# Choosing experts with plain float32 logits on four column groups, scales spread by a transfer, transposes issued together

## The chip, the core and the metric

The kernel runs on one core of a Trainium2 chip. The metric is the device time of one execution in microseconds. The kernel before takes 819.78 us (median of 3 runs, 819.25 to 821.07). The execution that the profiler recorded took 818.29 us, and its span, from the first to the last instruction, is 816.4 us.

## What is computed

The reference chains three layers over 4 sequences of 576 tokens with 512 features. First comes linear attention with 8 heads, then a feed-forward layer with a hidden size of 2048, then a layer with 8 experts of hidden size 1024. Only the last one's choice of experts is touched here:

```python
logits = np.einsum('bsd,de->bse', x, w_gate)
local_gate = 1.0 / (1.0 + np.exp(-np.einsum('bsd,de->bse', x, w_local).squeeze(-1)))
for b in range(B):
    prev_e = -1
    for s in range(S):
        fresh_e = int(np.argmax(logits[b, s]))
        if s == 0 or local_gate[b, s] < 0.5:
            e = fresh_e
        else:
            e = prev_e if prev_e >= 0 else fresh_e
        prev_e = e
        ...
        h = np.maximum(x[b, s] @ w1[e], 0.0)
        out[b, s] = p[e] * (h @ w2[e])
```

A token takes the expert of the token before it unless its gate is below one half. So nearly all tokens of a sequence share one expert. The result of each token is scaled by p[e], a softmax of the logits.

## The kernel before, in words

Features lie on the 128 partitions in four groups, tokens along the free dimension. The array `y` holds the stream of 4 x 2304 values per partition.

**Attention** (lines 426 to 479) runs in 29 steps, `attn_step`. Each loads keys and queries from memory on SP (`load_kq`, line 231, two buffers) and projects them (`proj`, line 292).

**Feed-forward and experts** are made of blocks (lines 511 and 512). The feed-forward layer has four units of five blocks of 432 or 480 tokens. Each sequence has two expert units, `g` 0 and 1, of two blocks of 288 tokens. Every product is made of three matmuls in float32r: high by high, low by high and high by low halves (`mm1`, lines 525 to 527; `mm2`, lines 544 to 546; output `psf`). `split_rows` (line 493) makes the halves of 288 tokens on ACT and POOL. The weights of an expert come as 8 pieces per unit. SP loads a piece into one of two raw buffers (line 153), ACT makes its high half (line 172) and DVE its low half (line 176).

**The order of work** is written out by hand. `work()` (line 747) goes through the blocks. Each block is 8 pieces of 12 matmuls, and after each piece comes a call of `side()` (line 705). That call does one step of a background list `bg` and prepares at most a few weight pieces. `route(b)`, a generator, is in that list, and each `yield` ends one step. It is appended in blocks 2, 3 and 4 of the last feed-forward unit for sequences 0, 1 and 2, and in the first expert block for sequence 3. While sequence 0 is not chosen, two steps are done per call. In `route(b)`:

- lines 574 to 578: both halves of the sequence are split, then three empty steps;
- line 586: 16 float32r matmuls of 288 columns give the logits (`glps`), from the split tokens and from the gate's weights as high and low half side by side (`wgr`, 18 columns); two copies to `r_gl`, line 587;
- line 593: five products with 18 rows (`lgps`) add the halves and put tokens on the partitions;
- lines 608 to 627: argmax, gate and softmax as small DVE instructions on `tr`;
- line 636: five transposes (`trps`), two in one step and three in the next, the last of 64 rows;
- lines 642 to 648: a scan along the tokens finds the kept expert; the probabilities are split into `r_th` and `r_tl`;
- line 650: POOL's queue writes both into `sall` on 32 of 64 partitions;
- lines 654 to 670: the most frequent expert is found (`cps` is a transpose of 8 counts), and `r_pm` marks the row to use.

`scale_row(b)` is put in front of `bg` at the start of an expert unit. Through `spread` it makes a selecting matrix on TensorE (`selps`, line 685) and two products with `sall` (`sbps`, line 691). They are copied to `sbc` (line 692), by which POOL multiplies the result (line 556). A loop after all that (from line 843) handles tokens whose expert differs. In the recorded execution it makes no pass.

Of the kernel before, what the change touches and what calls it, by code (L numbers as in the profile page):

```python
# [7 lines left out]
F32 = mybir.dt.float32  # L8
# [30 lines left out]
def model(ctx, tc, kq, vx, wphi, ident, up, vp, wff, wg, wmoe, rconst, outT):  # L39
# [8 lines left out]
    h_p = right.enter_context(tc.tile_pool(name="h", bufs=5, side="right"))  # L48
    ula_p = ctx.enter_context(tc.tile_pool(name="ula", bufs=1))
# [6 lines left out]
    wg_sb = const.tile([128, 4, 9], F32, name="wg_sb")  # L56
    wgr = const.tile([128, 4, 18], F32R, name="wgr")
# [512 lines left out]
    def route(b):  # L570

        ps_r, ul_p = late["psr"], late["ul"]
        lg, tr = late["lg"], late["tr"]
        for c in range(2):
            split_rows(b, c)
            yield
        for _ in range(3):
            yield

        gl = row(S, "r_gl")[:18]  # L580
        for c in range(2):
            sl = slice(c * CH, (c + 1) * CH)
            ps = ps_r.tile([18, CH], F32, tag="r1", bufs=2, name="glps")
            for k in range(4):
                for part in range(2):
                    nc.tensor.matmul(ps, lhsT=wgr[:, k], rhs=halves(b * S + c * CH, CH)[part][:, k], start=(k + part == 0), stop=(k + part == 4))  # L586
            nc.vector.tensor_copy(out=gl[:, sl], in_=ps)
            yield
        yield
        ps = ps_r.tile([128, 5, 9], F32, tag="r0", name="lgps")  # L590
        for c in range(5):
            m = 128 if c < 4 else 64
            nc.tensor.matmul(ps[:m, c], lhsT=gl[:, c * 128:c * 128 + m], rhs=rc_sb[:18, 104:113], start=True, stop=True)
# [34 lines left out]
        for _ in range(2):  # L628
            yield
        ta, tk, tp = (row(S, "r_t" + nm)[:8] for nm in "akp")  # L630
        for s0, cs in ((0, (0, 1)), (256, (2, 3, 4))):
            ps = ps_r.tile([72, 320], F32, tag="r1", bufs=2, name="trps")
            w = 0
            for c in cs:
                m = 128 if c < 4 else 64
                nc.tensor.transpose(ps[:, w:w + m], tr[:m, c], id_sb[:m, :m])
                w += m
            for n_, t in enumerate((ta, tk, tp)):
                nc.vector.tensor_copy(out=t[:, s0:s0 + w], in_=ps[32 * n_:32 * n_ + 8, :w])
            yield  # L640
# [5 lines left out]
        th, tl = (row(S, "r_t" + nm)[:8] for nm in "hl")  # L646
        nc.vector.tensor_copy(out=th.bitcast(F32R), in_=tp)
        nc.vector.tensor_tensor(out=tl.bitcast(F32R), in0=tp, in1=th, op=ALU.subtract)
        for n_, t in enumerate((th, tl)):
            nc.gpsimd.dma_start(out=late["sall"][32 * n_ + 8 * b:32 * n_ + 8 * b + 8], in_=t.bitcast(F32R))  # L650
        for _ in range(4):
            yield
# [14 lines left out]

        pm = ul_p.tile([1, 64], F32, tag=f"r_pm{b}", name="r_pm")
        nc.vector.tensor_scalar(out=pf, in0=pf, scalar1=float(8 * b), scalar2=None, op0=ALU.add)
        one_of_32(pm, pf)  # L670
        place[b] = pm
        pidx[b] = ix

    place = {}

    def one_of_32(dst, at_):

        nc.vector.tensor_scalar(out=dst.rearrange("p (a n) -> p a n", a=2), in0=iota32[0:1].unsqueeze(1).to_broadcast([1, 2, 32]),
                                scalar1=at_, scalar2=None, op0=ALU.is_equal)

    def spread(dst, pm):

        ps_r, ul_p, ones1, sall = (late[n] for n in ("psr", "ul", "ones1", "sall"))
        ps = ps_r.tile([64, 128], F32, tag="r1", bufs=2, name="selps")
        nc.tensor.matmul(ps, lhsT=pm, rhs=ones1, start=True, stop=True)
        sel = ul_p.tile([64, 128], F32R, tag="r_sel", name="r_sel")
        nc.vector.tensor_copy(out=sel, in_=ps)
        yield
        for c in range(2):
            ps = ps_r.tile([128, CH], F32, tag="r1", bufs=2, name="sbps")  # L690
            nc.tensor.matmul(ps, lhsT=sel, rhs=sall[:, c * CH:(c + 1) * CH], start=True, stop=True)
            nc.vector.tensor_copy(out=dst[:, c * CH:(c + 1) * CH], in_=ps)
            yield

    def scale_row(b):
        t = late["ul"].tile([128, S], F32, tag="sbc", name="sbc")
        scale[b] = t
        yield from spread(t, place[b])
# [16 lines left out]
    def side(i, step):  # L715

        u, _, _, c = blocks[i]
        if u.kind == "ffn":
            if splits and step in (2, 6):
                split_rows(*splits.pop(0))  # L720
            if u.g < 3:
                for _ in range(2 if step in (3, 7) else 1):
                    if not preps and room() and at["prep"] < min(8 * u.g + 16, 8 * u.g + 10 + 8 * c // 5 if u.g else 16):
                        preps.append(w_prep())
                    prep_step()
                if late:
                    w_ahead()
            else:
                if step == 0 and c > 1:
                    bg.append(route(c - 2))  # L730
                bg_step()
                if 0 not in pidx:
                    bg_step()
                if 0 in pidx and step in (1, 3, 4, 5, 7):
                    if at["prep"] < 8 * len(ffn_units) + 8 and room():
                        preps.append(w_prep())
                        drain(preps)
                        w_ahead()
        else:
            k = units.index(u)  # L740
            if u.b == 0 and u.g == 0 and c == 0 and step == 0:
                bg.append(route(3))
            bg_step()
            if c == 0 and step == 4 and u.g == 0:
                bg.insert(0, scale_row(u.b))
            if k + 1 < len(units) and at["prep"] < min(8 * (k + 2), 8 * k + 8 + 4 * c + (step + 1) // 2) and room():
                v = units[k + 1]
                if v.b not in pidx:
                    drain(bg)
                preps.append(w_prep())  # L750
                drain(preps)
                w_ahead()

    def work():

        for f in range(4):
            mm1(0, f)
            yield
        for i in range(n):
            u = blocks[i][0]  # L760
            if u.kind == "moe" and u.g == 1 and u.b not in scale:
                drain(bg)

            first = 3 if i == 1 else 0
            if i + 1 < n and not first:
                mm1(i + 1, 0)
            side(i, 0)
            yield
            for d in range(4):
                if first and d == first:  # L770
                    mm1(i + 1, 0)
                mm2(i, d)
                side(i, 1 + d)
                yield
            if i + 1 < n:
                for f in range(1, 4):
                    mm1(i + 1, f)
                    if f > 1:
                        store(1)
                    side(i, 4 + f)  # L780
                    yield
# [9 lines left out]
    def prepare(S_, late_):  # L791

        if (S_, late_) in ((1, 1), (2, 1), (3, 0), (4, 0)):
            next(early[0], "end")
        if late_ and S_ == W0:
            nc.vector.tensor_copy(out=wgr[:, :, 0:9], in_=wg_sb)
            nc.vector.tensor_tensor(out=wgr[:, :, 9:18], in0=wg_sb, in1=f32(wgr[:, :, 0:9]), op=ALU.subtract)
            w_dma()
        if S_ > W0:
            if S_ % 2 and late_ and at["prep"] < 8:  # L800
                preps.append(w_prep())
                w_ahead()
            prep_step()

    for S_ in range(NALL):
        if S_ == 1:
            nc.sync.dma_start(out=rc_sb, in_=rconst)
            nc.sync.dma_start(out=wg_sb, in_=wg)
        attn_step(S_)
# [7 lines left out]
    late["sall"] = ul_p.tile([64, S], F32R, name="sall")  # L817
# [10 lines left out]
    nc.gpsimd.memset(f32(late["sall"]), 0.0)  # L828
# [13 lines left out]
    with tc.For_i(0, nl):  # L842
# [3 lines left out]
        po = l_p.tile([1, 64], F32, name="l_po")  # L846
        be = l_p.tile([1, 2], F32, name="l_be")
        pl = l_p.tile([1, 4, 2], F32, name="l_pl")
        bi = l_p.tile([1, 6], I32, name="l_bi")
# [4 lines left out]
        one_of_32(po, pf)  # L854
        nc.vector.tensor_tensor(out=flags, in0=flags, in1=po[:, 0:32], op=ALU.subtract)
# [15 lines left out]
        nc.vector.tensor_copy(out=bi[:, 0:2], in_=be)  # L871
        nc.vector.tensor_copy(out=bi[:, 2:6], in_=pl[:, 0:2].rearrange("p a c -> p (a c)"))
        ev = nc.sync.value_load(bi[0:1, 1:2], min_val=0, max_val=NE - 1)
        bs = nc.sync.value_load(bi[0:1, 0:1], min_val=0, max_val=B - 1)
        bv = nc.vector.value_load(bi[0:1, 0:1], min_val=0, max_val=B - 1)
# [3 lines left out]
        for _ in spread(ls, po):  # L879
            pass  # L880
# [41 lines left out]
def layout(inputs):  # L922
# [41 lines left out]
    rc[0:18, 104:113] = np.concatenate([np.eye(9), np.eye(9)])  # L964
# [27 lines left out]
```

## Time and profile before

| what | value |
|---|---|
| median of 3 runs | 819.78 us |
| the profiled execution | 818.29 us |
| its span | 816.4 us |
| PE (TensorE matmul) busy | 797.6 us, 98% |
| DVE, ACT, POOL busy | 56%, 33%, 23% |
| TensorE clock granted, mean | 0.997 |

A line of a view names the engine, the line of the kernel, the operation, output and inputs by their names, partitions by elements, and a count. PE stands for matmuls, PEld for the loading of weights, SPq for the queue of SP. Matmuls are pipelined: the duration shown for one is longer than the distance to the next, so distances between starts tell what one costs in a stream.

### The profile page before, as it was taken

The numbers are of one execution on the slowest core, as the hardware profiler recorded it, in microseconds if no ns is written. First come the engines' busy times: TensorE is split into PE (matmuls) and PEld (weight loads), VectorE is DVE, ScalarE is ACT, GpSimd is POOL, SyncE is SP. The second block draws the span as 40 slices with busy tenths as digits, with TensorE's granted clock in tenths as the row PEclk, the third lists the DMA queues.
The fourth block names the chain that finished last, engine by engine and source line by source line (L and its number), as shares of the span: only waits on it lengthen the run. The fifth ranks groups of instructions, "written<-read, shape, count | busy, mean of one in ns | idle before, by whom it ended". The sixth has DMA issues, their size and how long they took to land.

```text
span 816.4 us, 17943 instructions
## 1 busy us (share of the span) xinstructions
PE 797.6 (98%) x7528; PEld 729.9 (89%) x7528; DVE 460.9 (56%) x913; ACT 267.5 (33%) x589; POOL 185.1 (23%) x242
## 2 busy tenths in 40 slices
PE   7999999999999999999999999999999999999995
PEld 5998889999888999889998899878899989999995
DVE  7899898732775453535545352247564847634332
ACT  5767776642311111111111111202233242333330
POOL 1122332100662221212212120023005232202011
PEclk9999999999999999999999999999999999999998
DMA  6434343100111110101101000002122322424311
GB/s 192 146 119 145 120 135 113 62 2 1 53 52 51 52 52 27 52 26 52 52 26 52 27 1 1 0 1 67 53 67 78 114 81 66 138 78 120 107 41 68
DMA packets 24676, 54.90 MB, mean 67 GB/s; under 512 B 3152, under 2 KB 8272, under 8 KB 24592
## 3 DMA queue, kind: packets, MB, share of 16 engines
q1 hardware_dynamic: 20304, 49.52, 19.4%
q10 hardware_dynamic: 4032, 4.05, 1.4%
q8 instruction: 61, 1.00, 0.5%
q0 software_dynamic: 256, 0.15, 0.1%
q14 instruction: 23, 0.19, 0.1%
HBM read 48.84 MB, written 4.72 MB: 66 GB/s over the span
## 4 chain that ended last, share of the span: by engine, by line
PE 90%; DVE 4%; ACT 2%; DMA 1%; issue 1%; POOL 1%; SPq 0%; DVEq 0%; ACTq 0%
PE psf L525 12%; PE psf L544 12%; PE psf L545 12%; PE psf L546 12%; PE psf L526 12%; PE psf L527 12%; PE kv L327 4%; PE pj L292 4%; PE num L361 3%; PE tq L341 2%; PE tps L387 1%; PE utps L404 1%; PE glps L586 1%; PE utps L399 1%; DMA kq<-in_kq 1%
## 5 line engine op out<-in xcount | busy, mean ns | idle before, releaser
L544 PE MATMUL psf<-hhi,w 128*128 128x288 f32 (+2 forms) x576 | 195.4, 339 | 0.5 <-ACT w L172 0.5
L545 PE MATMUL psf<-hhi,w 128*128 128x288 f32 (+2 forms) x576 | 194.3, 337 | 0.3 <-DVE w L176 0.3
L546 PE MATMUL psf<-hlo,w 128*128 128x288 f32 (+2 forms) x576 | 194.4, 337 | 0.0
L531 DVE SCALAR_TENSOR_TENSOR hlo<-psf,hhi 128x288 fp32r<-128x288 f32 (+2 forms) x144 | 80.0, 556 | 181.4 <-ACT hhi L530 181.2
L530 ACT ACTIVATE hhi<-psf 128x288 fp32r<-128x288 f32 (+2 forms) x144 | 70.8, 492 | 259.7 <-PE psf L527 256.1
L525 PE MATMUL psf<-hi_b,w 128*128 128x480 f32 (+1 forms) x352 | 120.8, 343 | 0.0
L526 PE MATMUL psf<-lo_b,w 128*128 128x480 f32 (+1 forms) x352 | 120.4, 342 | 0.1
L527 PE MATMUL psf<-hi_b,w 128*128 128x480 f32 (+1 forms) x352 | 119.9, 341 | 0.0
L544 PEld LDWEIGHTS psf<-hhi,w 128*128 128x128 f32 x576 | 108.2, 188 | 8.1 <-ACT w L172 0.8
L545 PEld LDWEIGHTS psf<-hhi,w 128*128 128x128 f32 x576 | 108.3, 188 | 7.2 <-DVE w L176 0.5
L553 DVE TENSOR_TENSOR y<-psf,y 128x480 f32<-128x480 f32 (+2 forms) x112 | 65.5, 585 | 87.1 <-PE psf L546 86.6
L546 PEld LDWEIGHTS psf<-hlo,w 128*128 128x128 f32 x576 | 108.2, 188 | 6.8
L75 POOL TENSOR_TENSOR cv_w<-cv_w,cv_b 128x256 f32<-128x256 f32 x64 | 45.9, 739 | 228.9 <-DVE cv_b L91 188.9
L525 PE MATMUL psf<-hi_a,w 128*128 128x432 f32 (+1 forms) x224 | 75.0, 335 | 0.0
L527 PE MATMUL psf<-hi_a,w 128*128 128x432 f32 (+1 forms) x224 | 74.1, 331 | 0.0
L526 PE MATMUL psf<-lo_a,w 128*128 128x432 f32 (+1 forms) x224 | 73.9, 330 | 0.0
L525 PEld LDWEIGHTS psf<-hi_b,w 128*128 128x128 f32 x352 | 66.1, 188 | 6.8 <-issue 0.5
L526 PEld LDWEIGHTS psf<-lo_b,w 128*128 128x128 f32 x352 | 66.1, 188 | 6.7 <-POOL lo_b L500 1.4
L527 PEld LDWEIGHTS psf<-hi_b,w 128*128 128x128 f32 x352 | 66.1, 188 | 5.2
L176 DVE TENSOR_TENSOR w<-raw,w 128x512 fp32r<-128x512 f32 x64 | 44.9, 701 | 29.8 <-ACT w L172 29.1
L172 ACT CAST w<-cv_w 128x512 fp32r<-128x512 f32 x32 | 19.9, 623 | 122.3 <-POOL cv_w L75 105.1
L556 POOL TENSOR_TENSOR y<-y,sbc 128x288 f32<-128x288 f32 x30 | 29.6, 988 | 133.2 <-DVE y L553 129.8
(139 smaller groups left out, 1151.4 us busy)
## 6 DMA issues: line engine op xcount, KB each, us to landing
raw<-in_wff SPq DMA_DIRECT2D x32, 512.0 KB, 3.3
raw<-in_wmoe SPq DMA_DIRECT2D x64, 256.0 KB, 2.7
kq<-in_kq SPq DMA_DIRECT2D x15, 576.0 KB, 4.1
vt<-in_vx SPq DMA_DIRECT2D x16, 325.0 KB, 3.0
outT<-y ACTq DMA_DIRECT2D x27, 144.0 KB, 3.0
outT<-y SPq DMA_DIRECT2D x5, 144.0 KB, 1.8
kq<-in_kq SPq DMA_DIRECT2D x2, 192.0 KB, 3.3
rawc<-in_up SPq DMA_DIRECT2D x1, 160.0 KB, 5.6
```

The costliest lines, as they stand in the source:

```text
L75: eng.tensor_tensor(out=dst[:, sl], in0=a[:, sl], in1=b[:, sl], op=op)
L176: nc.vector.tensor_tensor(out=w[:, 1], in0=f, in1=f32(w[:, 0]), op=ALU.subtract)
L292: nc.tensor.matmul(ps[c:c + 64, n_, i], lhsT=raw[g][r, t0 + c:t0 + c + 64], rhs=wphi_sb[r], start=True, stop=True)
L525: nc.tensor.matmul(ps, lhsT=wh, rhs=hi[:, k], start=(k == 0), stop=False)
L526: nc.tensor.matmul(ps, lhsT=wh, rhs=lo[:, k], start=False, stop=False)
L527: nc.tensor.matmul(ps, lhsT=wl, rhs=hi[:, k], start=False, stop=(k == 3))
L530: nc.scalar.activation(out=hhi, in_=ps, func=ACTF.Relu)
L531: nc.vector.scalar_tensor_tensor(out=hlo, in0=ps, scalar=0.0, in1=f32(hhi), op0=ALU.max, op1=ALU.subtract)
L544: nc.tensor.matmul(ps, lhsT=wh, rhs=hhi, start=(f == 0), stop=False)
L545: nc.tensor.matmul(ps, lhsT=wl, rhs=hhi, start=False, stop=False)
L546: nc.tensor.matmul(ps, lhsT=wh, rhs=hlo, start=False, stop=(f == 3))
L553: nc.vector.tensor_tensor(out=dst, in0=ps, in1=dst, op=ALU.add)
```

## The change

The logits come from `y` itself in plain float32. For each half of a sequence the four feature groups go to four groups of 32 output partitions, one matmul each. The gate's weights are padded with zeros to 32 columns. The five products that follow have 128 rows and add the four groups. The splits of the tokens move behind the logits (first half) and behind the softmax (second half). All five transposes are full and stand in one step. `route` has 16 steps where it had 21.

The probabilities go unsplit to memory on SP's queue, twice (`mine`, `sall`). The scale is loaded from `mine` by one SP transfer that repeats the chosen row on 128 partitions. `spread`, `one_of_32`, `selps` and `sbps` are gone. The load of the gate's weights stands outside of the `if`: it is issued ahead of every attention step.

```diff
-    wg_sb = const.tile([128, 4, 9], F32, name="wg_sb")
-    wgr = const.tile([128, 4, 18], F32R, name="wgr")
+    wg_sb = const.tile([128, 4, 32], F32, name="wg_sb")
...
-        for c in range(2):
-            split_rows(b, c)
-            yield
-        for _ in range(3):
-            yield
-
-        gl = row(S, "r_gl")[:18]
+        yield
+
+        gl = row(S, "r_gl")
         for c in range(2):
-            sl = slice(c * CH, (c + 1) * CH)
-            ps = ps_r.tile([18, CH], F32, tag="r1", bufs=2, name="glps")
+            ps = ps_r.tile([128, CH], F32, tag="r1", bufs=2, name="glps")
+            t0 = b * S + c * CH
             for k in range(4):
-                for part in range(2):
-                    nc.tensor.matmul(ps, lhsT=wgr[:, k], rhs=halves(b * S + c * CH, CH)[part][:, k], start=(k + part == 0), stop=(k + part == 4))
-            nc.vector.tensor_copy(out=gl[:, sl], in_=ps)
-            yield
+                nc.tensor.matmul(ps[32 * k:32 * k + 32], lhsT=wg_sb[:, k], rhs=y[:, k, t0:t0 + CH], start=True, stop=True)
+            nc.vector.tensor_copy(out=gl[:, c * CH:(c + 1) * CH], in_=ps)
+        yield
+        split_rows(b, 0)
+        yield
         yield
...
-            nc.tensor.matmul(ps[:m, c], lhsT=gl[:, c * 128:c * 128 + m], rhs=rc_sb[:18, 104:113], start=True, stop=True)
+            nc.tensor.matmul(ps[:m, c], lhsT=gl[:, c * 128:c * 128 + m], rhs=rc_sb[:, 104:113], start=True, stop=True)
...
-        for _ in range(2):
-            yield
+        yield
+        split_rows(b, 1)
+        yield
...
-            ps = ps_r.tile([72, 320], F32, tag="r1", bufs=2, name="trps")
+            ps = ps_r.tile([72, 384], F32, tag="r1", bufs=2, name="trps")
             w = 0
             for c in cs:
-                m = 128 if c < 4 else 64
-                nc.tensor.transpose(ps[:, w:w + m], tr[:m, c], id_sb[:m, :m])
-                w += m
+                nc.tensor.transpose(ps[:, w:w + 128], tr[:, c], id_sb)
+                w += 128
+            w = min(w, S - s0)
             for n_, t in enumerate((ta, tk, tp)):
                 nc.vector.tensor_copy(out=t[:, s0:s0 + w], in_=ps[32 * n_:32 * n_ + 8, :w])
-            yield
+        yield
...
-        th, tl = (row(S, "r_t" + nm)[:8] for nm in "hl")
-        nc.vector.tensor_copy(out=th.bitcast(F32R), in_=tp)
-        nc.vector.tensor_tensor(out=tl.bitcast(F32R), in0=tp, in1=th, op=ALU.subtract)
-        for n_, t in enumerate((th, tl)):
-            nc.gpsimd.dma_start(out=late["sall"][32 * n_ + 8 * b:32 * n_ + 8 * b + 8], in_=t.bitcast(F32R))
-        for _ in range(4):
+        yield
+
+        mine[b] = dram.tile([8, S], F32, name=f"mine{b}")
+        nc.sync.dma_start(out=mine[b], in_=tp)
+        nc.sync.dma_start(out=late["sall"][8 * b:8 * b + 8], in_=tp)
+        for _ in range(3):
             yield
...
     def scale_row(b):
-        t = late["ul"].tile([128, S], F32, tag="sbc", name="sbc")
-        scale[b] = t
-        yield from spread(t, place[b])
+
+        scale[b] = late["ul"].tile([128, S], F32, tag="sbc", bufs=2, name="sbc")
+        nc.sync.dma_start(out=scale[b], in_=mine[b][bass.ds(ereg[b], 1)].partition_broadcast(128))
...
             if c == 0 and step == 4 and u.g == 0:
-                bg.insert(0, scale_row(u.b))
+                scale_row(u.b)
...
         if late_ and S_ == W0:
-            nc.vector.tensor_copy(out=wgr[:, :, 0:9], in_=wg_sb)
-            nc.vector.tensor_tensor(out=wgr[:, :, 9:18], in0=wg_sb, in1=f32(wgr[:, :, 0:9]), op=ALU.subtract)
             w_dma()
...
     for S_ in range(NALL):
         if S_ == 1:
             nc.sync.dma_start(out=rc_sb, in_=rconst)
-            nc.sync.dma_start(out=wg_sb, in_=wg)
+            nc.gpsimd.memset(wg_sb[:, :, 9:32], 0.0)
+        nc.sync.dma_start(out=wg_sb[:, :, 0:9], in_=wg)
         attn_step(S_)
```

Left out are the loop for the tokens of other experts, the constants that pick the four groups, and the removed helpers' bodies.

## Rows read from the trace of the kernel before

**Rows 1.** Page, part 1: busy time of each engine, share of the span.
```profile
PE 797.6 (98%) x7528; PEld 729.9 (89%) x7528; DVE 460.9 (56%) x913; ACT 267.5 (33%) x589; POOL 185.1 (23%) x242
```
**Rows 2.** Busy time by stretch: PE, PEld, DVE, ACT, POOL, then clock, DMA.
```profile
585.00:640.00 55.00, 55.00 (x400) 52.49 (x399) 34.18 (x95) 20.81 (x44) 11.70 (x14) 1.00 0.26 77
```
**Rows 3.** Waits of PE: us in total, times, longest us.
```profile
PE psf L544 <- ACT w L172: 0.5, 1, 0.5
...
PE trps L636 <- DVE tr L627: 0.4, 1, 0.4
```
**Rows 4.** Timeline of PE: start us, us; two of the logits' matmuls.
```profile
577.59 0.29 PE L586 MATMUL glps<-hi_b,wgr 128*18 128x288 f32 x1
577.72 0.29 PE L586 MATMUL glps<-lo_b,wgr 128*18 128x288 f32 x1
```
**Rows 5.** Timeline of PE around the spreading of the scale.
```profile
602.09 0.29 PE L527 MATMUL psf<-hi_a,w 128*128 128x288 f32 x1
602.32 0.43 PE L685 MATMUL selps<-ones,r_pm 1*64 1x128 f32 x2
...
602.91 0.29 PE L526 MATMUL psf<-lo_a,w 128*128 128x288 f32 x1
...
604.23 0.29 PE L527 MATMUL psf<-hi_a,w 128*128 128x288 f32 x1
604.46 0.40 PE L691 MATMUL sbps<-sall,r_sel 64*128 64x288 f32 x1
...
605.02 0.29 PE L526 MATMUL psf<-lo_a,w 128*128 128x288 f32 x1
```
**Rows 6.** Timeline of PE around one tiny matmul in another tile form.
```profile
611.66 0.29 PE L546 MATMUL psf<-hlo,w 128*128 128x288 f32 x1
611.88 0.17 PE L654 MATMUL cps<-id_sb,r_cnt 8*1 8x8 f32 x1
...
612.21 0.29 PE L545 MATMUL psf<-hhi,w 128*128 128x288 f32 x1
```
**Rows 7.** Plain float32 matmuls: timeline of PE, and weight loads by line.
```profile
21.11 0.41 PE L266 MATMUL vps<-y 128*128 128x144 f32 x2
150.87 1.54 PE L292 MATMUL pj<-wphi_sb,kq 64*64 64x128 f32 x48
27.71 0.92 PE L327 MATMUL kv<-vt,ek 128*64 128x65 f32 x24
L327 PEld LDWEIGHTS kv<-vt,ek x1152: 132/138/139, 8.2 to 177.1; 128*64 128x64 f32 x192
```
**Rows 8.** Timeline of PE around the products that add the halves.
```profile
629.94 0.29 PE L546 MATMUL psf<-hlo,w 128*128 128x288 f32 x1
630.16 1.26 PE L593 MATMUL lgps<-rc_sb,r_gl 18*128 18x9 f32 x10
...
631.60 0.29 PE L526 MATMUL psf<-lo_a,w 128*128 128x288 f32 x1
```
**Rows 9.** Timeline of PE at the transposes.
```profile
593.44 0.38 PE L636 MATMUL trps<-id_sb,tr 128*72 128x128 f32 x2
...
595.25 0.56 PE L636 MATMUL trps<-id_sb,tr 128*72 128x128 f32 x3
...
595.97 0.30 PE L545 MATMUL psf<-hhi,w 128*128 128x288 f32 x1
```
**Rows 10.** Timeline of SP's queue and PE at the start.
```profile
5.97 0.71 SPq L808 DMA_DIRECT2D wg_sb<-in_wg  x1
7.89 0.33 SPq L231 DMA_DIRECT2D kq<-in_kq  x1
...
16.12 0.89 PE L292 MATMUL pj<-wphi_sb,kq 64*64 64x128 f32 x24
```
**Rows 11.** DMA issues: count, KB each, median us to landing.
```profile
kq<-in_kq SPq DMA_DIRECT2D x15, 576.0 KB, 4.1
...
wg_sb<-in_wg SPq DMA_DIRECT2D x1, 18.0 KB, 5.3
```

More of the change, by code (lines that the diff above doesn't have):

```diff
@@ L48, in model @@
     h_p = right.enter_context(tc.tile_pool(name="h", bufs=5, side="right"))
+    dram = ctx.enter_context(tc.tile_pool(name="dram", bufs=1, space=bass.MemoryType.DRAM))
     ula_p = ctx.enter_context(tc.tile_pool(name="ula", bufs=1))
@@ L666, in route @@
         nc.vector.tensor_tensor(out=late["flags"][:, 8 * b:8 * b + 8], in0=cr, in1=po, op=ALU.subtract)
[L668 to L671, printed above, removed]
         pidx[b] = ix
[L674 to L693, printed above, removed]
+    mine = {}
     def scale_row(b):
-        t = late["ul"].tile([128, S], F32, tag="sbc", name="sbc")
-        scale[b] = t
-        yield from spread(t, place[b])
+        scale[b] = late["ul"].tile([128, S], F32, tag="sbc", bufs=2, name="sbc")
+        nc.sync.dma_start(out=scale[b], in_=mine[b][bass.ds(ereg[b], 1)].partition_broadcast(128))
     bg = []
@@ L760, in work @@
             u = blocks[i][0]
-            if u.kind == "moe" and u.g == 1 and u.b not in scale:
-                drain(bg)
             first = 3 if i == 1 else 0
@@ L816, in model @@
     ul[1] = [ul_p.tile([128, 4, B * S - TA], F32R, name=n) for n in ("hi_b", "lo_b")]
-    late["sall"] = ul_p.tile([64, S], F32R, name="sall")
+    late["sall"] = dram.tile([8 * B, S], F32, name="sall")
     flags = late["flags"] = ul_p.tile([1, 32], F32, name="flags")
@@ L827, in model @@
     nc.gpsimd.memset(late["tr"], 0.0)
-    nc.gpsimd.memset(f32(late["sall"]), 0.0)
     for _ in todo:
@@ L845, in model @@
         pf = l_p.tile([1, 1], F32, name="l_pf")
-        po = l_p.tile([1, 64], F32, name="l_po")
+        po = l_p.tile([1, 32], F32, name="l_po")
         be = l_p.tile([1, 2], F32, name="l_be")
         pl = l_p.tile([1, 4, 2], F32, name="l_pl")
-        bi = l_p.tile([1, 6], I32, name="l_bi")
+        bi = l_p.tile([1, 7], I32, name="l_bi")
         tmp = l_p.tile([1, 16], F32, name="l_tmp")
@@ L853, in model @@
         nc.vector.tensor_copy(out=pf, in_=ix[:, 0:1])
-        one_of_32(po, pf)
-        nc.vector.tensor_tensor(out=flags, in0=flags, in1=po[:, 0:32], op=ALU.subtract)
+        nc.vector.tensor_scalar(out=po, in0=iota32[0:1], scalar1=pf, scalar2=None, op0=ALU.is_equal)
+        nc.vector.tensor_tensor(out=flags, in0=flags, in1=po, op=ALU.subtract)
         nc.vector.tensor_tensor(out=tmp, in0=po[:, 0:16], in1=po[:, 16:32], op=ALU.add)
@@ L871, in model @@
         nc.vector.tensor_copy(out=bi[:, 0:2], in_=be)
+        nc.vector.tensor_copy(out=bi[:, 6:7], in_=pf)
         nc.vector.tensor_copy(out=bi[:, 2:6], in_=pl[:, 0:2].rearrange("p a c -> p (a c)"))
@@ L874, in model @@
         bs = nc.sync.value_load(bi[0:1, 0:1], min_val=0, max_val=B - 1)
+        rs = nc.sync.value_load(bi[0:1, 6:7], min_val=0, max_val=8 * B - 1)
         bv = nc.vector.value_load(bi[0:1, 0:1], min_val=0, max_val=B - 1)
@@ L878, in model @@
         ls = l_p.tile([128, S], F32, name="l_s")
-        for _ in spread(ls, po):
-            pass
+        nc.sync.dma_start(out=ls, in_=late["sall"][bass.ds(rs, 1)].partition_broadcast(128))
         yb = l_p.tile([128, 4, S], F32, name="l_y")
@@ L963, in layout @@
     rc[:, 8:40] = np.arange(32)
-    rc[0:18, 104:113] = np.concatenate([np.eye(9), np.eye(9)])
+    for r in range(0, 128, 32):
+        rc[r:r + 9, 104:113] = np.eye(9)
     rc[:, 40:104] = np.concatenate([np.eye(64), np.eye(64)])
```

## The prediction

> **What bounds the kernel now.** I read the page's busy shares first: TensorE is busy 797.6 of 816.4 us [rows 1]. A share over the whole span can hide stages, so I read the stretch in which most of the routing runs. There PE is busy 55.00 of 55.00 us, while DVE has 34.18, ACT 20.81 and POOL 11.70 [rows 2]. The list of PE's waits then shows what is late where. In the last 300 us there is one wait of 0.4 us at a transpose of the routing and a late pair for expert weights, of which the longer is 0.5 us [rows 3]. So routing work costs time almost wherever PE itself does it, and nearly nothing where another engine does it. The question is how much PE time the change takes out, and whether it puts a wait in.
>
> **How a piece is priced.** In an unbroken stream, matmuls of 288 columns start 0.13 us apart [rows 4]. The cost of a foreign piece is the distance from the stream matmul ahead of it to the second stream matmul behind it, less two such distances of 0.13. Going to the second catches the delay that the first one still carries.
>
> **Scale through memory, removed from PE.** The two `selps` cost 602.91 - 602.09 - 0.26 = 0.56 us. Each `sbps` costs 605.02 - 604.23 - 0.26 = 0.53 us, and there are two [rows 5]. That is 1.62 us for a sequence and **6.5 us** for four. What replaces it is one transfer on SP, issued at step 4 of the sequence's first expert block. Its reader is POOL's multiplication in the second expert unit, over one and a half blocks later. A block is 96 matmuls of 0.13, so 12.5 us, and the cover is some 18 us. It carries 128 rows of 2.3 KB, 295 KB in all. Keys of 576 KB land in 4.1 us [rows 11]. I cost it at nothing. If the cover were gone, POOL and the result's stores would wait, not PE.
>
> **The transfers of SP.** Each sequence adds two writes and the broadcast to the queue that also fetches expert weights. The writes wait for DVE's product of the probabilities, and weight loads queue behind them. That product is issued one step earlier, and a weight load waits for a DVE subtraction that stands later in DVE's order, so the hold ends first. Once the weights were late all the same [rows 3], so this chain has little slack. Its pair of waits, at most 2 x 0.5 = 1 us, can vanish or recur. I take 0 and keep -1 to +2 us. POOL loses its two issues for a sequence and DVE seven instructions. Neither bounds [rows 2], so zero.
>
> **Logits.** Today 16 matmuls at 0.13 us make 2.1 us a sequence, with no visible price for entering or leaving [rows 4]. The new form has 8 plain float32 matmuls. The trace shows each such matmul as two instructions: two of 144 columns are (0.41 - 0.29) = 0.12 us apart when they run alone [rows 7]. So 288 columns take 0.24 us each, and 16 of them would be 3.84 us, if one ran after the other. They need not. The projections, on four 64 by 64 tiles, put 48 instructions into 1.54 us: (1.54 - 0.27)/47 = 0.027 us apart. One of their 128 columns alone would take 0.12 x 128/144 = 0.11, so four run side by side. On two column groups with all 128 rows, `kv` has (0.92 - 0.22)/23 = 0.030 us for 65 columns, where one alone would be 0.055, so two run side by side [rows 7]. Four column groups with 128 rows are not in the trace. The bounds are one and four at a time. I take four, because every tiled form shown reaches the full number of its tiles. Then it is 4 rounds of 0.24, or 0.96 us. The tile form is new to the stream around it, so I add a trip into another form and back. The tiny `cps` prices that: 612.21 - 611.66 - 0.26 = 0.29 us [rows 6]. Both halves stand in one step, so one trip: 1.25 us against 2.1, a gain of **3.3 us** for four sequences.
>
> Here a rule speaks against the change. The Trainium skill, page "TensorE: Matmul & The Clock Gate", section "Part 3: Packing small matmuls — row/col tiling", says a weight load overlaps running matmuls only where the row groups differ. The four column groups share all rows, so by it each round would show its load. With 0.13 us for a load of 64 columns [rows 7], that is at most 16 rounds x 0.13 = 2.1 us more. The trace bears the rule out badly: `kv` shares all rows too, its loads last 0.138 us, and its instructions still start 0.030 us apart.
>
> **Products behind the logits.** `lgps` costs 631.60 - 629.94 - 0.26 = 1.40 us [rows 8]. It takes 18 rows today, and its first load stands 0.22 us behind the stream matmul. With 128 rows the way in is no change of form. I take off half a trip, 0.15 us, so **0.6 us** for four. The last product still has 64 columns, so the way out stays.
>
> **Transposes.** Two cost 2 x (0.38 - 0.27) = 0.22 us. The three, with a short one of 64 rows, cost 595.97 - 595.25 - 0.13 = 0.59 [rows 9], since nothing stands between them and the stream ahead. Five full ones are 0.55 against 0.81, so **1.0 us** for four. For sequence 0 the wait of 0.4 us [rows 3] came because DVE's chain followed an `mm1` piece with its two evictions. Now it follows an `mm2` piece with one addition, and the next piece is 12 x 0.22 = 2.6 us long. I count **0.4 us** gained; the bound on the other side is 0.
>
> **The start.** The load of the gate's weights is now issued 29 times on SP, each into the place of the one before, in short pieces. If each must wait until its predecessor has landed, the keys queue behind it. Today that load landed 5.3 us after issue [rows 11], and keys were issued at 7.89 for a projection at 16.12 [rows 10]. In the new order the first stands one place earlier, so issued near 5.5 and landed near 10.8. With the second's 0.7 on SP the keys go out at 11.5 to 12 and land 4.1 later, about 16. That costs between 0 and 1 us; I take **0.3**. Later keys are issued a full pair ahead of use, so 28 further issues cost nothing unless they grow (third rival).
>
> **Sum.** 6.5 + 3.3 + 0.6 + 1.0 + 0.4 - 0.3 = 11.5 us. The profiled execution took 818.29 us, so 806.8. The median of the runs lies 1.5 us above it, which gives **808.3 us**.
>
> **Rivals.**
>
> *Fewer groups at a time.* With two side by side the logits take 8 x 0.24 + 0.29 = 2.2 us a sequence. They gain nothing, and the time is 812.1. With loads not hidden behind the round before it is 808.3 + 2.1 = 810.4; that is what the rule of the Trainium skill's page "TensorE: Matmul & The Clock Gate" would make of it. For it: the form is not shown. Against it: `pj` and `kv`.
>
> *Groups one after the other.* 3.84 + 0.29 = 4.1 us, 2.9 us a sequence more than I take. That is 11.5 us in all, and it eats the whole gain: 819.8, no change. Against it stands every tiled row [rows 7].
>
> *The repeated load paces attention, slower.* Each of the loads waits for the one before, and SP holds the keys behind it. The weight loads of `kv` run from 8.2 to 177.1 us [rows 7] over 24 steps, 7.0 us a step. So this decides from the point where a load takes longer than about 7 us from issue to landing. Beyond it every one of 24 steps is stretched to the landing. At 8 us that is 1.0 x 24 = 24 us, and 832. For it: 5.3 us are seen for one load of long pieces [rows 11], and four times as many pieces are asked for. Against it: that load was queued behind the first keys and values and would not be later. The Trainium skill, page "DMA: Bandwidth & Descriptors", section "Two DMAs through the same engine are not ordered", asks for such a wait on the first transfer; no row here shows one.
>
> *The change does less than it says.* The weights' late pair [rows 3] repeats in each sequence because SP now also writes. At 1 us a sequence that is +4, so 812.
>
> **Chances.** Forecast 0.70; fewer groups or open loads 0.13; one after the other 0.04; paced attention 0.06; late weights 0.07. A measurement of this kernel tells 0.2% (1.6 us) from no change. Faster is the first, second and last, less a little: 0.88. Same is 0.05. Slower is 0.07. The forecast's own span is 806 (the late pair gone, nothing at the start) to 810. To hold 8 in 10 the range reaches to 813.
>
> **What would show it.** Right: no `selps` and `sbps`; `glps` instructions in fours, a sequence's 16 within 1.3 us; five transposes within 0.6; PE as full as before from 560 us on. Wrong: `glps` starts 0.24 or 0.12 us apart; new waits of `psf` on weights, or of `pj` on `kq`, by over 1 us in total.

## The result and the profile after

The changed kernel takes 812.4 us (median of 6 runs, 810.59 to 815.76), against 819.9 us before. The ratio is 0.9912, 95% interval 0.989 to 0.9934: faster by 7.5 us. The forecast was 808.3 us, with a range to 813. So the direction and the range held, and 4 us of the gain are missing. The profiled execution took 813.27 us and has a span of 811.5 us, where before it was 818.29 and 816.4.

What was taken off TensorE is gone. The timeline of PE in the changed kernel (start us, us) shows the logits, the products behind them and the transposes:

```profile
555.82 0.38 PE L546 MATMUL psf<-hlo,w 128*128 128x480 f32 x1
556.13 1.18 PE L581 MATMUL glps<-y,wg_sb 128*32 128x288 f32 x16
...
557.57 0.38 PE L545 MATMUL psf<-hhi,w 128*128 128x480 f32 x1
...
578.46 0.71 PE L633 MATMUL trps<-id_sb,tr 128*72 128x128 f32 x5
...
579.23 0.38 PE L545 MATMUL psf<-hhi,w 128*128 128x480 f32 x1
...
601.10 0.29 PE L546 MATMUL psf<-hlo,w 128*128 128x288 f32 x1
601.23 1.17 PE L590 MATMUL lgps<-rc_sb,r_gl 128*128 128x9 f32 x10
...
602.56 0.30 PE L526 MATMUL psf<-lo_a,w 128*128 128x288 f32 x1
```

By the same reckoning as in the prediction (480 columns are 0.22 us apart), a sequence's logits cost 557.57 - 555.82 - 0.44 = 1.31 us against 2.1 [rows 4]. The products behind them cost 602.56 - 601.10 - 0.26 = 1.20 against 1.40 [rows 8]. The five transposes cost 579.23 - 578.46 - 0.22 = 0.55 against 0.81 [rows 9].

What came instead stands in the list of PE's waits of the changed kernel (us in total, times, longest):

```profile
PE psf L545 <- DVE w L176: 2.3, 2, 1.5
...
PE psf L544 <- ACT w L172: 1.5, 1, 1.5
PE trps L633 <- DVE tr L624: 1.0, 1, 1.0
```

Waits for expert weights were 0.8 us and are 3.8 us. Before, they were the 0.5 us of [rows 3] and this line:

```profile
PE psf L545 <- DVE w L176: 0.3, 1, 0.3
```

The first transposes wait 1.0 us, where it was 0.4 [rows 3]. The busy time by stretch (columns as in [rows 2]) shows a third loss, behind the wait at 624 us:

```profile
624.00:628.00 4.00, 2.47 (x20) 0.95 (x19) 2.78 (x10) 1.67 (x2) 0.79 (x1) 0.80 0.41 131
628.00:632.00 4.00, 4.00 (x24) 4.00 (x25) 1.48 (x3) 0.62 (x1) 0.84 (x2) 0.77 0.21 66
```

The granted clock was 0.80 and 0.77 in two stretches of 4 us. With levels of 1 and one half that is (0.20 + 0.23) x 4 / 0.5 = 3.4 us at half clock (1.2 instead of 2.4 GHz). There the stream's matmuls of 288 columns start 0.24 us apart (628.26 and 628.50) instead of 0.13, so about half of it, 1.7 us, was lost. Of the six timed executions four have a mean granted clock of 0.997 or 0.998 and two have 0.995 and 0.992, so this loss need not be in each of them.

Why the weights were late stands in SP's timeline and in DVE's, side by side (start us, us):

```profile
617.00 0.32 SPq L647 DMA_DIRECT2D mine<-r_tp  x1
617.36 0.32 SPq L648 DMA_DIRECT2D sall<-r_tp  x1
617.91 2.14 SPq L153 DMA_DIRECT2D raw<-in_wmoe  x2
...
613.55 0.72 DVE L176 TENSOR_TENSOR w<-raw,w 128x512 fp32r<-128x512 f32 x1
614.19 1.34 DVE L640 TENSOR_TENSOR_SCAN r_ta<-r_tk,r_ta 8x576 f32<-8x576 f32 x1
...
616.23 0.74 DVE L643 TENSOR_TENSOR r_tp<-r_tp,r_ta 8x576 f32<-8x576 f32 x1
616.90 0.67 DVE L176 TENSOR_TENSOR w<-raw,w 128x512 fp32r<-128x512 f32 x1
```

The DVE subtraction that ends at 614.27 frees a raw buffer, so the next weight piece could be fetched then. But SP stands at the write to `mine` until the probabilities are done at 616.97, and the piece goes out at 617.91, 3.6 us late. ACT and DVE stand for it, and with them the work on the piece behind it. The low half of that second piece, done at 625.54, is what PE waits for at 624 us (ACT, DVE and PE, start us, us):

```profile
621.76 0.62 ACT L172 CAST w<-raw 128x512 fp32r<-128x512 f32 x1 [3.76 <-DMA raw<-in_wmoe]
622.41 0.69 DVE L176 TENSOR_TENSOR w<-raw,w 128x512 fp32r<-128x512 f32 x1 [3.92 <-ACT w L172]
...
624.85 0.69 DVE L176 TENSOR_TENSOR w<-raw,w 128x512 fp32r<-128x512 f32 x1
625.59 0.40 PE L545 MATMUL psf<-hhi,w 128*128 128x288 f32 x1 [1.53 <-DVE w L176]
```

This was sequence 2. For sequence 3 the write goes out at 650.10, and the waits near 656 us follow. For sequences 0 and 1 the list has no wait of PE on weights.

### The profile page after: what moved, and what is told of

It is laid out like the page before. It is cut to its first block, busy times and chain, and to the rows that moved or that the text cites. A ratio compares the mean times of both kernels' runs of the same rounds, so it can differ in the third digit from the quotient of the medians.

```text
span 811.5 us, 17916 instructions
## 1 busy us (share of the span) xinstructions
PE 790.5 (97%) x7512; PEld 725.6 (89%) x7512; DVE 449.1 (55%) x883; ACT 267.0 (33%) x589; POOL 179.1 (22%) x234
## 4 chain that ended last, share of the span: by engine, by line
PE 91%; DVE 4%; ACT 2%; DMA 1%; issue 1%; ACTq 0%; POOL 0%; SPq 0%; DVEq 0%
PE psf L544 12%; PE psf L525 12%; PE psf L545 12%; PE psf L546 12%; PE psf L527 12%; PE psf L526 12%; PE kv L327 4%; PE pj L292 4%; PE num L361 3%; PE tq L341 2%; PE tps L387 1%; PE utps L404 1%; PE utps L399 1%; DMA raw<-in_wmoe 1%; DVE pg L297 1%
```

## Experiments

**The hold on SP.** The first edit sends the writes out on POOL's queue, at the same step:

```diff
-        nc.sync.dma_start(out=mine[b], in_=tp)
-        nc.sync.dma_start(out=late["sall"][8 * b:8 * b + 8], in_=tp)
+        nc.gpsimd.dma_start(out=mine[b], in_=tp)
+        nc.gpsimd.dma_start(out=late["sall"][8 * b:8 * b + 8], in_=tp)
```

> The changed kernel with one edit: the two writes of the probabilities go out on POOL's queue instead of SP's. Theory (hold): in the changed kernel SP stands at the first write until DVE has finished the scan, 3.6 and 3.3 us after the next expert weight could have been fetched, and that weight is what PE waits for. Without the hold the waits of psf on w fall from 3.8 us to under 1 us, no stretch inside the kernel has a granted clock of one half, and the time falls by 3 to 5 us against the changed kernel, to 807.5 to 809.5. Rival (load): the weights are late because the routing's DVE work or the extra transfers fall together with them; then the waits stay at 3 to 4 us and the time at about 812.

The second leaves them on SP and issues them two steps later:

```diff
+        for _ in range(2):
+            yield
         mine[b] = dram.tile([8, S], F32, name=f"mine{b}")
         nc.sync.dma_start(out=mine[b], in_=tp)
         nc.sync.dma_start(out=late["sall"][8 * b:8 * b + 8], in_=tp)
-        for _ in range(3):
-            yield
+        yield
```

> The changed kernel with one edit: the two writes stay on SP's queue but are issued two steps later. Theory (hold): DVE has finished the probabilities by then, so SP does not stand; waits of psf on w under 1 us, time 807.5 to 809.5, as with POOL's queue. Rival (the queue itself: two more transfers beside the weights): the waits stay, since the same transfers are on the same queue; about 812.

Measured: 809.57 us on POOL's queue (ratio 0.9862, 0.9848 to 0.9876), just over what was expected, and 808.48 us two steps later (0.985, 0.9838 to 0.9863). The second run was made once more with the last one below, and gave 808.80 (0.9871, 0.9854 to 0.9887).

> The run with the later writes alone once more, on the chip of the run above, for the comparison: 808.5 us within 0.7, ratio 0.985.

In both forms no wait of `psf` on `w` is left, and the profile shows no half clock between 14 and 800 us. The four longest waits of PE with the later writes:

```profile
PE pj L292 <- DMA wphi_sb<-in_wphi: 3.2, 1, 3.2
PE kv L327 <- ACT kvs L331: 2.1, 4, 0.9
PE pj L292 <- DVE cv_a L84: 1.1, 1, 1.1
PE trps L633 <- DVE tr L624: 1.0, 1, 1.0
```

The same transfers on the same queue do no harm once they stand elsewhere in its order. So it was the hold, not the extra traffic. For sequence 2 the piece now goes out as soon as DVE's subtraction has ended, at 615.58:

```profile
614.87 0.71 DVE L176 TENSOR_TENSOR w<-raw,w 128x512 fp32r<-128x512 f32 x1
615.61 0.33 SPq L153 DMA_DIRECT2D raw<-in_wmoe  x1
```

One detail came out otherwise than expected: SP still stands. Its timeline with the later writes, sequence 3:

```profile
644.59 0.33 SPq L153 DMA_DIRECT2D raw<-in_wmoe  x1
647.92 0.35 SPq L649 DMA_DIRECT2D mine<-r_tp  x1
...
648.88 0.38 SPq L153 DMA_DIRECT2D raw<-in_wmoe  x1
```

The weight piece that the hold delayed is now ahead of the writes (644.59). The piece behind them (648.88) loses nothing, since its buffer comes free only at 648.86, when a DVE subtraction of 0.67 us that starts at 648.19 has ended.

**One part of the change alone.** To the kernel before, only the scale through memory was added, with the later writes:

```diff
-        th, tl = (row(S, "r_t" + nm)[:8] for nm in "hl")
-        nc.vector.tensor_copy(out=th.bitcast(F32R), in_=tp)
-        nc.vector.tensor_tensor(out=tl.bitcast(F32R), in0=tp, in1=th, op=ALU.subtract)
-        for n_, t in enumerate((th, tl)):
-            nc.gpsimd.dma_start(out=late["sall"][32 * n_ + 8 * b:32 * n_ + 8 * b + 8], in_=t.bitcast(F32R))
-        for _ in range(4):
+        for _ in range(2):
+            yield
+        mine[b] = dram.tile([8, S], F32, name=f"mine{b}")
+        nc.sync.dma_start(out=mine[b], in_=tp)
+        nc.sync.dma_start(out=late["sall"][8 * b:8 * b + 8], in_=tp)
+        for _ in range(2):
             yield
...
-        yield from spread(t, place[b])
+        nc.sync.dma_start(out=scale[b], in_=mine[b][bass.ds(ereg[b], 1)].partition_broadcast(128))
```

> The kernel before with one part of the change alone: the scale through memory (writes on SP two steps behind the scan, broadcast load), all else as before. Theory: PE loses selps and sbps, 6.4 us by the distances in the trace, and nothing takes their place, so 820.3 - 6.4 = 813.9, 813 to 815. Rival: the transfers are paid for elsewhere (late weights, late scale) and the gain is under 4 us.

Measured: 811.03 us, ratio 0.9892 (0.9877 to 0.9906), so 7.7 to 10.1 us less and under the 813 to 815 that were expected. Alone, and without the hold on SP, it does as much as the whole change. The distances between PE's matmuls give 6.4 us, as expected. PE's weight waits also fell, from 0.8 to 0.5 us:

```profile
PE psf L546 <- DVE w L177: 0.5, 1, 0.5
PE trps L637 <- DVE tr L628: 0.4, 1, 0.4
```

Its profiled execution was 7.1 us shorter (811.17 against 818.29). The timed runs have 1.8 us beyond that, because the profiled execution of the kernel before was 1.7 us faster than their median of 819.97. What the profiled executions have beyond the 6.4 and the shorter waits was not found.

**Four column groups or one.** The four matmuls of a half now accumulate in one group of 32 output partitions:

```diff
-        gl = row(S, "r_gl")
+        gl = row(S, "r_gl")[:32]
...
-            ps = ps_r.tile([128, CH], F32, tag="r1", bufs=2, name="glps")
+            ps = ps_r.tile([32, CH], F32, tag="r1", bufs=2, name="glps")
...
-                nc.tensor.matmul(ps[32 * k:32 * k + 32], lhsT=wg_sb[:, k], rhs=y[:, k, t0:t0 + CH], start=True, stop=True)
+                nc.tensor.matmul(ps, lhsT=wg_sb[:, k], rhs=y[:, k, t0:t0 + CH], start=(k == 0), stop=(k == 3))
...
-            nc.tensor.matmul(ps[:m, c], lhsT=gl[:, c * 128:c * 128 + m], rhs=rc_sb[:, 104:113], start=True, stop=True)
+            nc.tensor.matmul(ps[:m, c], lhsT=gl[:, c * 128:c * 128 + m], rhs=rc_sb[:32, 104:113], start=True, stop=True)
```

> The changed kernel with one edit: the four feature groups of the logits accumulate in one group of 32 output partitions instead of going to four. Theory: the four column groups run side by side; in one group 16 instructions start 0.24 us apart, 3.84 us and a trip of 0.29 for a sequence against 1.31 in the changed kernel, so about 2.8 us a sequence and 11 us in all, some 823 (waits may differ by 2 us). Rival: the column form gains little and the 0.24 us is hidden elsewhere; then under 4 us more.

Measured: 827.08 us, ratio 1.0078 (1.0063 to 1.0092), slower than the kernel before and 4 us above what was expected. Its timeline of PE:

```profile
602.80 0.29 PE L546 MATMUL psf<-hlo,w 128*128 128x288 f32 x1
603.02 4.07 PE L581 MATMUL glps<-y,wg_sb 128*32 128x288 f32 x16
...
607.26 0.29 PE L545 MATMUL psf<-hhi,w 128*128 128x288 f32 x1
```

The 16 instructions start (4.07 - 0.41)/15 = 0.24 us apart, and a sequence costs 607.26 - 602.80 - 0.26 = 4.20 us. Side by side it was 1.31. Four times the difference is 11.6 us. The rest of the 14.7 us by which it is slower than the changed kernel includes products behind that are again in another form (1.39 us a sequence), and in this profile 6.8 us at half clock behind its weight waits, which cost some 3.4 us.

**The first transposes' wait.** The split of the second half moves behind the transposes:

```diff
         yield
-        split_rows(b, 1)
         yield
         ta, tk, tp = (row(S, "r_t" + nm)[:8] for nm in "akp")
...
+        split_rows(b, 1)
         nc.vector.tensor_tensor_scan(out=ta, data0=tk, data1=ta, initial=0.0, op0=ALU.mult, op1=ALU.add)
```

> The changed kernel with one edit: the split of a sequence's second half moves from ahead of the transposes to behind them. Theory: for sequence 0 POOL's four subtractions run beside DVE's small steps ahead of the transposes and stretch three of them from 0.16, 0.20 and 0.17 us to 0.34, 0.65 and 0.70 us, so the transposes wait 1.0 us. With the split behind, these steps take 0.16 to 0.20 us again and the wait is under 0.2 us; 1 us less than the changed kernel. Rival: the chain of DVE steps is too long for its place whatever POOL does; the wait stays over 0.4 us.

DVE's steps ahead of the transposes in the changed kernel, with POOL's split beside them:

```profile
539.14 0.34 DVE L615 TENSOR_SCALAR r_fr<-lg 128x5 f32<-128x5 f32 x1
...
539.63 0.65 DVE L617 TENSOR_TENSOR tr<-tr,r_fr 128x40 f32<-128x40 f32 x1
540.31 0.70 DVE L618 TENSOR_SCALAR r_fr<-r_fr 128x5 f32<-128x5 f32 x1
...
537.88 3.10 POOL L500 TENSOR_TENSOR lo_a<-y,hi_a 128x288 fp32r<-128x288 f32 x4 [4.86 <-ACT hi_a L498]
```

And with the split moved, when POOL is idle:

```profile
540.53 0.16 DVE L615 TENSOR_SCALAR r_fr<-lg 128x5 f32<-128x5 f32 x1
...
540.84 0.20 DVE L617 TENSOR_TENSOR tr<-tr,r_fr 128x40 f32<-128x40 f32 x1
541.08 0.17 DVE L618 TENSOR_SCALAR r_fr<-r_fr 128x5 f32<-128x5 f32 x1
```

The steps have their plain lengths again and the wait is gone from the list. Measured: 811.28 us, ratio 0.9899 (0.9886 to 0.9912). That is 1.1 us under the changed kernel's median, but the intervals overlap; the profile decides here. The hold on SP is still in this version, and its weight waits of 3.2 us were not followed by half clock.

**The repeated load.** The load of the gate's weights goes back into the `if` and is issued once:

```diff
-        nc.sync.dma_start(out=wg_sb[:, :, 0:9], in_=wg)
+            nc.sync.dma_start(out=wg_sb[:, :, 0:9], in_=wg)
         attn_step(S_)
```

> The changed kernel with one edit: the gate's weights are loaded once, in the second attention step, instead of 29 times. Theory: the repeated loads only move the start; the last projections start 0.3 us later in the changed kernel than before. So 0.2 to 0.5 us less than the changed kernel's 812.4, which its own runs can't tell, and SP's 29 us of waiting on these loads is gone. Rival (the loads hold the keys): over 1.5 us less, and projections earlier from step to step.

Measured: 813.2 us, ratio 0.9926 (0.9912 to 0.994), no less than the changed kernel. SP waits 28.8 us for these loads in the changed kernel, but nobody waits for SP there. The first of the logits' matmuls starts at 528.1 us in the changed kernel and at 529.3 in this one:

```profile
L581 PE MATMUL glps<-y,wg_sb x64: 405/407/688, 528.1 to 627.2; 128*32 128x288 f32 x64
```
```profile
L581 PE MATMUL glps<-y,wg_sb x64: 406/406/430, 529.3 to 627.3; 128*32 128x288 f32 x64
```

So 28 of 29 loads cost nothing that can be seen.

**The edits together.** Later writes, the split behind the transposes for all sequences, and one load:

> The changed kernel with three edits together: writes of the probabilities two steps later on SP, the second split behind the transposes, the gate's weights loaded once. Theory: the three are separate, 812.4 - 3.9 - 1.1 - 0.3 = 807.1 us, with no wait of PE over 0.2 us behind 200 us of the span. Rival: an edit uncovers another wait; then 808.5 or more.

Measured: 808.86 us, ratio 0.9868 (0.9854 to 0.9883), no better than the later writes alone, as the rival had it. The same with the writes on POOL's queue:

> As the run of the three edits, but the writes go out on POOL's queue at their old step. Theory: the hold is what counts, not the queue, so the same 807.1 us within 0.7. Rival: POOL stands at the write instead and its splits or multiplications come late; over 808 us.

Measured: 810.29 us, 0.9883 (0.9869 to 0.9897), also over what was expected. The first run's profile shows why the edits don't add up. ACT's and POOL's timelines around sequence 3:

```profile
647.25 3.82 ACTq L567 DMA_DIRECT2D outT<-y  x4
651.18 0.41 ACT L530 ACTIVATE hhi<-psf 128x288 fp32r<-128x288 f32 x1 [3.58 <-DMA outT<-y]
651.48 0.61 ACT L172 CAST w<-raw 128x512 fp32r<-128x512 f32 x1
...
644.70 5.24 POOL L500 TENSOR_TENSOR lo_b<-y,hi_b 128x288 fp32r<-128x288 f32 x4
649.91 1.55 POOL L556 TENSOR_TENSOR y<-y,sbc 128x288 f32<-128x288 f32 x2
```

The moved split now stands on POOL ahead of the multiplication of finished results. ACT stands at their stores for 3.6 us. Behind them are its activations and the high half of a weight piece, and PE waits 0.3 us for a high and 0.8 us for a low half. With the writes on POOL's queue ACT stands at the stores as long, and PE waits 1.3 us. So the split was moved for sequence 0 alone:

```diff
         yield
-        split_rows(b, 1)
+        if b:
+            split_rows(b, 1)
         yield
...
+        if not b:
+            split_rows(b, 1)
         nc.vector.tensor_tensor_scan(out=ta, data0=tk, data1=ta, initial=0.0, op0=ALU.mult, op1=ALU.add)
```

> The changed kernel with three edits: the writes two steps later, the gate's weights loaded once, and the split of the second half behind the transposes for sequence 0 only. In the run with that split moved for all four sequences, POOL did the last one ahead of the multiplications of finished results, ACT stood at their stores and the weights came late. Theory: with the other three splits at their old place that wait is gone too, PE has no wait over 0.2 us behind 200 us, and the time is 0.5 to 1.5 us under the run with the later writes alone. Rival: the wait near 652 us comes back wherever the split is; then the same time as that run or more.

Measured: 807.54 us, ratio 0.9853 (0.9837 to 0.987). PE's list has no wait of `trps` or `psf` left, and from 560 to 760 us PE is never idle:

```profile
560.00:760.00 200.00, 200.00 (x1449) 194.25 (x1448) 106.62 (x250) 70.09 (x147) 44.02 (x48) 1.00 0.34 98
```

The time is under both kernels' times. In the same set of runs it is 1.3 us under the later writes alone, though the intervals overlap.

## Why the prediction was right and wrong

**The scale off PE** (6.5 us) was right: 6.4 by distances, and alone it moved the time by at least that. The broadcast landed 3.1 us after its issue, and nothing waited for it.

**The logits** (3.3 us) were right: (2.10 - 1.31) x 4 = 3.2. The choice between one and four groups at a time decided the sign: 827.08 us is the other end. The rounds of four start (1.18 - 0.41)/3 = 0.26 us apart, against 0.24 for one instruction alone in the run with one group. So at most 0.02 us a round is left for weight loads, though each of the 64 instructions has its own, of 0.11 us:

```profile
L581 PEld LDWEIGHTS glps<-y,wg_sb x64: 106/110/178, 528.1 to 626.8; 128*32 128x32 f32 x64
```

The prediction's 2.1 us for open loads counted one load a round, where there are four. The rule on row groups from the Trainium skill's page "TensorE: Matmul & The Clock Gate", section "Part 3: Packing small matmuls — row/col tiling", does not hold here.

**The products behind** (0.6) and **the transposes** (1.0) were right: (1.40 - 1.20) x 4 = 0.8 and (0.81 - 0.55) x 4 = 1.0. No run has either of them alone, so they are shown by distances only.

**The wait for sequence 0** was wrong. It was to fall from 0.4 to 0 and rose to 1.0 us. The step counted which piece of PE's work lies ahead, but not what POOL does meanwhile. ACT is free there and does its part of the moved split from 536.66 us on, so POOL's subtractions (from 537.88) fall on DVE's chain and stretch three of its steps by 1.2 us in all. With the split moved, the wait was gone, so the place that the prediction chose was right by itself.

**The transfers of SP** were the step that failed most. "The hold ends first" compared the wrong two subtractions. The weight load behind the write doesn't wait for the subtraction that follows the scan in DVE's order, but for the one ahead of it, which had ended 2.7 us before the probabilities. The term of 0 with bounds of -1 to +2 us was 3.0 us of further waits in the profile, and behind one of them 1.7 us lost at half clock. That is over its upper bound, and 812.4 us is inside the range only because the rivals had stretched it to 813. The fourth rival named this, late weights because SP also writes, with 812 us and a chance of 0.07; it came in. But it had 1 us in each of four sequences, where longer waits came in two and half clock made up the rest, so its exact time is partly luck. Without the hold the times are near the forecast of 808.3: 808.48 and 808.80 us with the later writes and 809.57 on POOL's queue, all with the wait for sequence 0 still in them.

**The start** (0.3) can't be told from nothing, and the third rival, loads that pace attention, is out: their median landing is 3.1 us, well under the 7.0 of a step.

In the profiled executions: 6.4 + 3.2 + 0.8 + 1.0 = 11.4 us off PE, less 0.6, 3.0 and 1.7, leaves 6.1. The span fell by 4.9. The remaining 1.2 us were not followed further.

## What to carry to other kernels

A DMA moved to another queue brings its wait along: look for what stands behind it in that queue's program order, and when exactly that could have gone. Where PE is full, price a foreign piece by the distance between the stream matmuls on its two sides, and put small products on separate column groups. An early start of one engine's work can hurt another's chain: the split was worth moving for one sequence and cost as much when moved for all.

## What the runs showed of the hardware that was not expected

Granted clock fell to half for 3.4 us after a PE wait of 1.5 us in the changed kernel. With the split moved, a wait of 1.4 us at the same place was followed by full clock:

```profile
624.00:628.00 4.00, 2.64 (x27) 1.65 (x26) 3.45 (x11) 1.68 (x2) 0.80 (x1) 1.00 0.48 131
628.00:632.00 4.00, 4.00 (x33) 4.00 (x32) 1.77 (x4) 0.62 (x1) 2.51 (x3) 1.00 0.24 66
```

In the changed kernel itself PE stood for longer near 656 us, in two waits of 1.5 and 0.8 us, and the clock stayed full:

```profile
656.00:660.00 4.00, 1.75 (x11) 1.35 (x10) 2.00 (x8) 1.82 (x5) 0.00 (x0) 1.00 0.61 180
```

So the same kind of wait can cost twice its length or just its length. What decides it is not shown here.

DVE instructions on as little as 128 x 5 elements took 0.70 instead of 0.17 us while POOL subtracted. The Trainium skill, page "SBUF — State Buffer", section "Terms", says DVE and GpSimd share a port pair that one holds for a whole instruction while the other stands. The rows above agree: the stretched steps, up to 0.53 us longer, are within one POOL subtraction of 3.10/4 = 0.78 us.
